# Two token groups hand the last two of their eight units to a fourth block of fast products

## The chip, the cores and the metric

The kernel runs on one core of a Trainium2 chip. The metric is the device time of one execution in microseconds (us). The engines are TensorE (PE, matmuls, with its weight loads as PEld), VectorE (DVE), ScalarE (ACT), GpSimd (POOL) and SyncE (SP), which issues nearly all DMAs. Each engine works through its own queue in order.

## What is computed

Attention with a window and with a dilated window for 8 batches, 8 heads, 576 positions and a head size of 64, then a gated MLP over the 4608 tokens of width 512, with 2048 hidden values:

```python
rel = pos[:, None] - pos[None, :]
mask_plain = (rel >= 0) & (rel < window)                       # window = 32
mask_dil = (rel >= 0) & (rel < window * dilation) & (rel % dilation == 0)
...
attn = np.exp(scores)
attn = attn / (np.sum(attn, axis=-1, keepdims=True) + 1e-09)
return np.matmul(attn, v).astype(np.float32)
...
h = x @ w_in
g = h * (1.0 / (1.0 + np.exp(-1.702 * h)))
return (g @ w_out).astype(np.float32)
```

## The kernel before

The sums are kept in float32 by splitting each operand into a high and a low part: a product is three matmuls (high by high, low by high, high by low) of 128x128 weights and 512 columns.

**Tokens.** Each batch has 576 tokens. The first 512 of a batch make a group of 512 columns; the last 64 of all eight batches make a ninth. Attention is done in 32 pieces k, four for a batch (k = 4b to 4b + 3, two heads each): `scores` (PE, into the bank sp), mask, maximum, subtraction and sum (DVE), exponential (ACT), division (POOL or DVE), transposes (DVE), eight copies into the one buffer bt (ACT or DVE), `product` (PE, into the bank av) and the copy of x out of the bank. In a row of the profile sp is the scores and av the product.

**Groups.** `ALONE` is 3: the groups of batches 0, 1 and 2 (class `Group`, names m0, m1, m2) are multiplied directly. The 2048 hidden values are NF = 16 chunks f of 128. For a chunk, `up` makes hp with 12 matmuls (line 863), ACT and DVE make the gate (lines 871 and 872) and split it into gh and gl, and `Down.pieces` multiplies it onto the four banks acc with 12 matmuls (lines 800, 801, 804). After the last chunk `add_out` stores the group's result. While PE multiplies a chunk, the other engines do the attention of later batches.

**Weight sums.** After group 0, `sum_weights` and `sum_out_weights` make, for each of the PAIRS = 8 units u (chunks u and u + 8 together), the seven combinations of the weights that the blocks need, and store them to DRAM (`sums`, `sums_o`). They work in the arena units 0 to 3 and 4 to 7, one unit u after the other. The eighth (u = 7) adds over wi_last.

**Blocks.** The other six groups are multiplied two at a time by class `Block`: p has the batches 3 and 4, q has 5 and 6, r the ninth group and 7. With two groups of tokens and two chunks of hidden values a product of 2x2 parts is made by seven products in place of eight. `sum_tokens` loads the tokens from `tokens_x`, sums them and splits the seven sums into `wi_kept`, two slots each. The sums for p use the arena units 0 to 11, so the units of the weight sums have to be free, and the slots of wi_kept need every weight sum to be done. Then `products_` goes through the eight units: `up` (42 matmuls a unit, line 1006, seven loads of 256 KB from `sums`), gates, `operands` (sums and splits into wo_kept), and after every second unit `second_products` (84 matmuls, line 1121, seven loads of 512 KB from `sums_o` through a ring of four slots). `add_to` adds the banks to the result units on DVE (line 1142) and stores a finished one.

**Order.** Nothing is scheduled by hand: every step is given to `Plan` with its cost on each engine that can do it and its urgency. `placed` puts the steps in an order by these costs, choosing the engine that would finish first; `latest` gives each step a due time from that order, and three more rounds place them by due times. So the order of all engines is one list made ahead, and each engine's queue is fixed in it.

Of the kernel before, what the change touches and what calls it, by code (L numbers as in the profile page):

```python
# [17 lines left out]
P = 128  # L18
# [5 lines left out]
ALONE = 3  # L24
NSUM = 14
# [191 lines left out]
def tile_windowed_attention_then_gated_mlp(  # L217
# [64 lines left out]
    tokens_x = dram.tile([B * NC, P, GT], F32, tag="tokens_x", name="tokens_x")  # L282
    tokens_r = dram.tile([NC, P, B * LT], F32, tag="tokens_r", name="tokens_r")
# [329 lines left out]
    def drain_x(k, urgency):  # L613
# [53 lines left out]
        if b >= ALONE:  # L667
            add({DMA: 262}, urgency, lambda e: load(tokens_x[k], to), [f"{name}.{n}" for n in range(5)], (f"tx{k}",))
# [115 lines left out]
    class Down:  # L784


        def __init__(self, name, dest):
            self.name, self.dest = name, dest
            self.acc = {}

        def pieces(self, f, high, low, need):
# [4 lines left out]
            def hi(j):  # L796
                if f == 0:
                    self.acc[j] = quarter(j, f"acc_{self.name}_{j}")
                cols = slice(P * j, P * j + P)
                T.matmul(self.acc[j], w[:, 0, cols], high, start=f == 0, stop=False)  # L800
                T.matmul(self.acc[j], w[:, 1, cols], high, start=False, stop=False)  # L801

            def lo(j):
                T.matmul(self.acc[j], w[:, 0, P * j:P * j + P], low, start=False, stop=f == NF - 1)  # L804
# [7 lines left out]
            if f != NF - 1:  # L812
# [3 lines left out]
        def add_out(self, j):  # L816
# [5 lines left out]
            def store(e):  # L822
                load(dst, arena[:, at].rearrange("p (b s) -> p b s", b=dst.shape[1]))

            add({ACT: 0.48, DVE: 0.6}, -9.0, drain, (f"acc{j}",), own(at))
            add({DMA: 262}, -9.0, store, (f"A{at}",), ())
# [5 lines left out]
    class Group:  # L832


        def __init__(self, name, dest):
            self.name = name
            self.g, self.hps = {}, {}
            self.down = Down(name, dest)
# [115 lines left out]
    class Block:  # L954


        def __init__(self, name, sources, dests, units, few=False):
            self.name, self.sources, self.dests, self.few = name, sources, dests, few
# [126 lines left out]
        def second_products(self, chunk):  # L1085
# [14 lines left out]
            def groups(b, n, place, begins, to):  # L1100
                slot = None

                def half(j):
# [4 lines left out]
                    key, fresh = keys[where][j], begins and (where != "R" or chunk == 0)  # L1108
# [49 lines left out]

        def products_(self):


            for u in range(PAIRS):
                self.up(u)
                ops = self.operands(u)
                if u % 2 == 0 and u:
# [35 lines left out]
    for i in range(4):  # L1201
# [3 lines left out]
    main = [Group(f"m{b}", dests[b]) for b in range(ALONE)]  # L1205
# [4 lines left out]
              Block("r", (B, 7), (dests[B], dests[7]), late_units)]  # L1210
# [11 lines left out]
    for b, g in enumerate(main):  # L1222
# [16 lines left out]
        for f in range(NF):  # L1239
# [6 lines left out]
    for block in blocks:  # L1246
        block.sum_tokens()
        if block.few:
# [64 lines left out]
```

## Time and profile before

| | |
|---|---|
| time, median of 3 runs | 823.12 us (821.65 to 823.53) |
| the profiled execution | 822.45 us, span 820.7 us |
| PE busy | 809.3 us, 99% of the span |
| DVE, ACT, POOL busy | 669.0, 518.0, 328.4 us |
| granted TensorE clock | 0.997 |
| DMA | 188.13 MB in the span, 229 GB/s on average |

The span is the time from the first to the last instruction. Busy times of engines overlap. In a row of the timeline the columns are the start and the length in us, the engine, the line of the kernel, the operation, what is written and read, the count, and in brackets the idle time before it with what ended it. In the windows, each engine's busy microseconds and count stand in the order PE, PEld, DVE, ACT, POOL, then the granted clock, the DMA engines' busy share and GB/s.

### The profile page before, as it was taken

The numbers are of one execution on the slowest core, as the hardware profiler recorded it, in microseconds if no ns is written. First come the engines' busy times: TensorE is split into PE (matmuls) and PEld (weight loads), VectorE is DVE, ScalarE is ACT, GpSimd is POOL, SyncE is SP. The second block draws the span as 40 slices with busy tenths as digits, with TensorE's granted clock in tenths as the row PEclk, the third lists the DMA queues.
The fourth block names the chain that finished last, engine by engine and source line by source line (L and its number), as shares of the span: only waits on it lengthen the run. The fifth ranks groups of instructions, "written<-read, shape, count | busy, mean of one in ns | idle before, by whom it ended". The sixth has DMA issues, their size and how long they took to land.

```text
span 820.7 us, 18890 instructions
## 1 busy us (share of the span) xinstructions
PE 809.3 (99%) x7279; PEld 653.4 (80%) x7279; DVE 669.0 (82%) x1081; ACT 518.0 (63%) x988; POOL 328.4 (40%) x294
## 2 busy tenths in 40 slices
PE   7999999999999999999999999999999999999997
PEld 4677878888887888778888888888888888888886
DVE  6898988888888876899889899996679885867575
ACT  7898986767577766786866654545456534544340
POOL 3442325455556553244345445531215332112251
PEclk9999999999999999999999999999999999999999
DMA  9577658899758657797788777775565658674545
GB/s 354 186 249 212 175 161 296 287 318 303 241 176 271 223 180 243 252 307 234 235 236 264 253 254 249 234 256 183 179 207 189 198 189 275 201 226 157 180 153 181
DMA packets 109610, 188.13 MB, mean 229 GB/s; under 512 B 26448, under 2 KB 55376, under 8 KB 109520
## 3 DMA queue, kind: packets, MB, share of 16 engines
q1 hardware_dynamic: 109376, 186.78, 70.2%
q8 instruction: 58, 0.95, 0.5%
q14 instruction: 32, 0.26, 0.1%
q10 hardware_dynamic: 144, 0.13, 0.0%
HBM read 140.64 MB, written 45.09 MB: 226 GB/s over the span
## 4 chain that ended last, share of the span: by engine, by line
PE 97%; DMA 1%; DVE 1%; issue 0%; ACT 0%; SPq 0%; DVEq 0%
PE hp_m L863 16%; PE up_p L1006 10%; PE up_r L1006 9%; PE up_q L1006 9%; PE acc_m L800 5%; PE second_p_Q L1121 5%; PE second_q_Q L1121 5%; PE acc_m L804 5%; PE acc_m L801 5%; PE second_r_Q L1121 5%; PE sp L490 4%; PE second_q_Z L1121 3%; PE second_r_Z L1121 3%; PE second_R L1121 3%; PE second_p_Z L1121 3%; PE av L608 2%
## 5 line engine op out<-in xcount | busy, mean ns | idle before, releaser
L353 POOL TENSOR_TENSOR arena<-arena 128x256 f32<-128x256 f32 (+3 forms) x94 | 100.7, 1083 | 97.8 <-DVE wi_last_units L353 21.6
L863 PE MATMUL hp_m<-xs,wi_kept 128*128 128x512 f32 x504 | 127.7, 396 | 1.2 <-DVE arena L872 0.9
L863 PEld LDWEIGHTS hp_m<-xs,wi_kept 128*128 128x128 f32 x504 | 92.9, 188 | 22.8 <-DVE arena L872 1.9
L353 POOL TENSOR_TENSOR wo_kept<-arena,wo_kept 128x512 fp32r<-128x512 f32 x41 | 56.9, 1395 | 131.5 <-ACT wo_kept L346 84.9
L346 ACT ACTIVATE wo_kept<-arena 128x512 fp32r<-128x512 f32 x111 | 69.2, 630 | 40.7 <-PE second_r_Q L1121 10.9
L1006 PE MATMUL up_r<-wi_kept,xs 128*128 128x512 f32 x336 | 85.3, 389 | 0.0
L1006 PE MATMUL up_p<-wi_kept,xs 128*128 128x512 f32 x336 | 84.2, 394 | 0.2 <-DVE arena L353 0.2
L1006 PE MATMUL up_q<-wi_kept,xs 128*128 128x512 f32 x336 | 83.4, 389 | 0.0
L1006 PEld LDWEIGHTS up_p<-wi_kept,xs 128*128 128x128 f32 x336 | 62.1, 188 | 14.7 <-DVE arena L353 0.9
L1006 PEld LDWEIGHTS up_q<-wi_kept,xs 128*128 128x128 f32 x336 | 63.0, 188 | 13.3 <-DVE arena L1028 0.3
L1006 PEld LDWEIGHTS up_r<-wi_kept,xs 128*128 128x128 f32 x336 | 63.1, 188 | 13.1
L353 DVE TENSOR_TENSOR wo_kept<-arena,wo_kept 128x512 fp32r<-128x512 f32 x80 | 61.1, 775 | 5.1 <-ACT wo_kept L346 4.7
L346 ACT ACTIVATE bt<-ct 32x256 f32<-32x256 f32 (+1 forms) x130 | 56.6, 435 | 11.7 <-DVE ct L534 6.0
L353 POOL TENSOR_TENSOR pr<-pr,sm 128x320 f32<-128x320 f32 x52 | 43.7, 856 | 48.5 <-DVE sm L518 43.5
L800 PE MATMUL acc_m<-gh,wo_kept 128*128 128x512 f32 x156 | 61.5, 394 | 0.0
L353 POOL TENSOR_TENSOR wo_kept<-wi_last_units,wo_kept 128x512 fp32r<-128x512 f32 x22 | 29.9, 1361 | 78.3 <-ACT wo_kept L346 72.3
L353 DVE TENSOR_TENSOR arena<-arena 128x512 f32<-128x512 f32 (+1 forms) x75 | 59.1, 797 | 2.7 <-ACT arena L346 1.8
L801 PE MATMUL acc_m<-gh,wo_kept 128*128 128x512 f32 x156 | 60.8, 390 | 0.0
L1027 ACT ACTIVATE arena<-arena 128x512 f32<-128x512 f32 x60 | 37.4, 628 | 33.4 <-DVE arena L353 27.2
L1028 DVE SCALAR_TENSOR_TENSOR arena<-arena 128x512 f32<-128x512 f32 x60 | 49.8, 837 | 1.7 <-ACT arena L1027 1.3
L346 ACT ACTIVATE gh<-arena 128x512 fp32r<-128x512 f32 x57 | 36.0, 631 | 17.5 <-DVE arena L872 5.8
L353 DVE TENSOR_TENSOR gl<-arena,gh 128x512 fp32r<-128x512 f32 x53 | 41.3, 779 | 6.5 <-ACT gh L346 3.2
(267 smaller groups left out, 1824.7 us busy)
## 6 DMA issues: line engine op xcount, KB each, us to landing
xs<-sums SPq DMA_DIRECT2D x168, 256.0 KB, 3.3
out_weights<-sums_o SPq DMA_DIRECT2D x63, 512.0 KB, 3.5
qk<-qk_dram SPq DMA_DIRECT2D x29, 576.0 KB, 4.4
xs<-sums_o SPq DMA_DIRECT2D x21, 512.0 KB, 3.8
v<-vp_dram SPq DMA_DIRECT2D x28, 320.0 KB, 4.1
sums_o<-arena SPq DMA_DIRECT2D x32, 256.0 KB, 3.2
sums<-arena SPq DMA_DIRECT2D x32, 256.0 KB, 2.9
arena<-wi_dram SPq DMA_DIRECT2D x15, 512.0 KB, 4.7
```

Source lines behind the costliest of these rows:

```text
L346: A.activation(dst, src, AF.Copy, scale=scale)
L353: (V if e == DVE else G).tensor_tensor(out=dst, in0=a, in1=b, op=op)
L490: T.matmul(dst[:, w:w + n], u["qk"][rows, at:at + 32], u["qk"][rows, S + first:S + first + n], start=not masked(k), stop=True, tile_positi ...
L608: T.matmul(u["x"][i][rows, at:at + last - first], u["v"][keys, a, m], bt[keys, m, a, first:last], start=(bank_, a) not in begun, stop=True ...
L800: T.matmul(self.acc[j], w[:, 0, cols], high, start=f == 0, stop=False)
L801: T.matmul(self.acc[j], w[:, 1, cols], high, start=False, stop=False)
L804: T.matmul(self.acc[j], w[:, 0, P * j:P * j + P], low, start=False, stop=f == NF - 1)
L863: T.matmul(hps[f], wi(f)[:, st, cols], mv[:, c], start=c == 0 and k == 0, stop=c == NC - 1 and k == 2)
L1006: T.matmul(self.banks[place], xs[:, slot, at:at + P], wi_kept[:, 2 * a + c, mv], start=fresh and c == 0 and k == 0, stop=c == 1 and k == 2 ...
L1027: add({ACT: 0.60}, -10.0, lambda e: A.activation(unit(tmp), src(), AF.Tanh, scale=0.851), need, own(tmp))
L1028: add({DVE: -0.70 if need[0][0] == "A" else 0.70}, -10.0, lambda e: V.scalar_tensor_tensor(out=unit(dst), in0=unit(tmp), scalar=1.0, in1=s ...
L1121: T.matmul(self.second[key], w[:, st, cols], mv, start=fresh and y == 0 and k == 0, stop=y == 1 and k == 2, skip_group_check=True)
```

## The change

The groups of batches 1 and 2 leave out the chunks whose unit is 6 or 7 (f = 6, 7, 14, 15; `BOTH` is 2) and store what they have to a new DRAM buffer `partial` in place of the output. Their tokens are now also stored to `tokens_x`, as those of later batches are. A fourth block, s, takes the two groups' tokens through units 6 and 7 alone, by the seven products, after r. `begin_with` loads the partial sums into the result units, so that `add_to` adds to them.

```diff
-        if b >= ALONE:
+        if b > 0:
             add({DMA: 262}, urgency, lambda e: load(tokens_x[k], to), [f"{name}.{n}" for n in range(5)], (f"tx{k}",))
...
             def store(e):
-                load(dst, arena[:, at].rearrange("p (b s) -> p b s", b=dst.shape[1]))
+                if self.part is not None:
+                    load(partial[self.part + j], arena[:, at])
+                else:
+                    load(dst, arena[:, at].rearrange("p (b s) -> p b s", b=dst.shape[1]))
...
+            self.fs = [f for f in range(NF) if b == 0 or f % PAIRS < PAIRS - BOTH]
+            self.down = Down(self.name, dests[b], self.fs, NC * (b - 1) if b else None)
...
+        def begin_with(self, first):
+
+
+            for q in range(4):
+                for j in range(2):
+                    at, n = RESULTS[q][j], first + NC * (q // 2) + 2 * (q % 2) + j
+                    self.touched.add((q, j))
+                    add({DMA: 262}, -3.0, lambda e, at=at, n=n: load(unit(at), partial[n]), (f"part{n}",), own(at))
...
-            for u in range(PAIRS):
+            for u in self.us:
...
-              Block("r", (B, 7), (dests[B], dests[7]), late_units)]
+              Block("r", (B, 7), (dests[B], dests[7]), late_units),
+              Block("s", (1, 2), (dests[1], dests[2]), late_units, us=range(PAIRS - BOTH, PAIRS))]
...
-        for f in range(NF):
+        for f in g.fs:
             g.up(f)
...
+        if block is blocks[-1]:
+            block.begin_with(0)
```

The rest of the diff passes the first and last chunk of a group on to the banks' start and stop, and lets block s begin its banks R at its own first pair of units. Since the planner makes the order anew, it changes from group 1 on. Lines of the changed kernel are 3 to 7 higher than those of the kernel before (1006 is now 1013, 608 is 611, 353 is 356).

**The entry into block p on PE.** Before, the queue has this where group 2 ends and p begins; acc_m2 belongs to group 2, up_p_0_0 and up_p_0_1 are the first products of p:

```order
L800 MATMUL acc_m2_3_3497<-gh1_74,wo_last_71 128x512
L801 MATMUL acc_m2_3_3497<-gh1_74,wo_last_71 128x512
L804 MATMUL acc_m2_0_3484<-gl1_76,wo_last_71 128x512
L804 MATMUL acc_m2_1_3487<-gl1_76,wo_last_71 128x512
L804 MATMUL acc_m2_2_3493<-gl1_76,wo_last_71 128x512
L804 MATMUL acc_m2_3_3497<-gl1_76,wo_last_71 128x512
L800 MATMUL acc_m2_0_3484<-gh0_73,wo_last_71 128x512
L801 MATMUL acc_m2_0_3484<-gh0_73,wo_last_71 128x512
L1006 MATMUL up_p_0_0_4600<-wi_kept_68,xs_72 128x512 x6
L1006 MATMUL up_p_0_1_4611<-wi_kept_68,xs_72 128x512 x3
L800 MATMUL acc_m2_1_3487<-gh0_73,wo_last_71 128x512
```

The products of p begin while the group's last chunk and a half still have to be multiplied onto acc. In the changed kernel the rows ahead of up_p are these; the last acc_m2 stands 15 rows above the first of them, right behind the matmuls of sp_24 and av_22, with sp_25 and av_23 and the first two rows of av_24 between:

```order
L611 MATMUL av_24_4296<-bt_77,v_24_4260 64x96 x10
L611 MATMUL av_24_4296<-bt_77,v_24_4260 64x64 x2
L611 MATMUL av_24_4296<-bt_77,v_24_4260 64x32 x2
L611 MATMUL av_24_4296<-bt_77,v_24_4260 64x64 x4
L493 MATMUL sp_26_4333<-qk_26_4266 32x64 x36
L611 MATMUL av_25_4393<-bt_77,v_25_4325 64x96 x2
L611 MATMUL av_25_4393<-bt_77,v_25_4325 64x32 x2
L611 MATMUL av_25_4393<-bt_77,v_25_4325 64x96 x10
L611 MATMUL av_25_4393<-bt_77,v_25_4325 64x64 x2
L611 MATMUL av_25_4393<-bt_77,v_25_4325 64x32 x2
L611 MATMUL av_25_4393<-bt_77,v_25_4325 64x64 x4
L1013 MATMUL up_p_0_1_4434<-wi_kept_68,xs_72 128x512 x3
```

No multiplication of a group is left between; the pieces 24 and 25 of attention stand ahead of p.

**The same place on DVE.** Before, the sums and splits of p's tokens (arena from arena, wi_kept from arena) stand among the gates of group 2's chunks 14 and 15 and one mask of attention:

```order
L353 TENSOR_TENSOR wi_kept_68<-arena_78,wi_kept_68 128x512
L353 TENSOR_TENSOR arena_78<-arena_78 128x512
L872 SCALAR_TENSOR_TENSOR arena_78<-arena_78,hp_m2_14_4459 128x512
L534 STREAM_TRANSPOSE ct1_92<-pr1_84 128x2x5x32
L353 TENSOR_TENSOR pr0_83<-sp_26_4487,mask_97 128x2x4x64
L534 STREAM_TRANSPOSE ct1_92<-pr1_84 128x2x5x32
L353 TENSOR_TENSOR pr0_83<-sp_26_4487,mask_97 64x2x64
L510 TENSOR_REDUCE mx0_85<-pr0_83 128x10
L353 TENSOR_TENSOR wi_kept_68<-arena_78,wi_kept_68 128x512
L353 TENSOR_TENSOR gl0_75<-arena_78,gh0_73 128x512
L353 TENSOR_TENSOR arena_78<-arena_78 128x512
L353 TENSOR_TENSOR wi_kept_68<-arena_78,wi_kept_68 128x512
```

In the changed kernel the last of the weight sums' adds (arena from wi_last) is followed by the mask of sp_24, and the work of attention piece 24 by that of 25 and 26:

```order
L356 TENSOR_TENSOR gl1_76<-arena_78,gh1_74 128x512
L356 TENSOR_TENSOR arena_78<-arena_78 128x512
L356 TENSOR_TENSOR arena_78<-wi_last_69 128x512
L356 TENSOR_TENSOR pr0_84<-sp_24_4079,plain_99 128x2x4x64
L356 TENSOR_TENSOR pr0_84<-sp_24_4079,plain_99 64x2x64
L513 TENSOR_REDUCE mx0_86<-pr0_84 128x10
L351 COPY arena_78<-av_22_4116 128x2x16
L351 COPY arena_78<-sp_24_4079 128x16 x2
L356 TENSOR_TENSOR pr0_84<-pr0_84,mx0_86 128x10x64
L351 COPY bt_77<-arena_78 32x8x32
L353 TENSOR_SCALAR arena_78<-acc_m2_2_3068 128x512
```

42 instructions further on from the mask of sp_24, the first split that a product of p waits for is the first of the four in this piece:

```order
L356 TENSOR_TENSOR pr0_84<-pr0_84,mx0_86 128x10x64
L356 TENSOR_TENSOR wi_kept_68<-arena_78,wi_kept_68 128x512
L529 TENSOR_REDUCE sm0_89<-pr0_84 128x10
L356 TENSOR_TENSOR arena_78<-arena_78 128x512
L521 RECIPROCAL sm0_89<-sm0_89 128x10
L356 TENSOR_TENSOR arena_78<-arena_78 128x512
L356 TENSOR_TENSOR wi_kept_68<-arena_78,wi_kept_68 128x512 x4
L537 STREAM_TRANSPOSE ct0_92<-pr0_84 128x2x5x32 x2
L356 TENSOR_TENSOR wi_kept_68<-arena_78,wi_kept_68 128x512
L356 TENSOR_TENSOR arena_78<-arena_78 128x512
L356 TENSOR_TENSOR wi_kept_68<-arena_78,wi_kept_68 128x512
```

No gate of a group is among them any more; the mask of sp_24, at the head of the 42, reads matmuls that stand just ahead of the last acc_m2.

**The end on SP.** Before, the last loads of weights for r (out_weights, xs) are followed by the stores of the results and by nothing else:

```order
L1096 DMA out_weights_4830<-sums_o_80 128x1024 x3
L1096 DMA xs_72<-sums_o_80 128x1024
L1096 DMA out_weights_4830<-sums_o_80 128x1024 x3
L1096 DMA xs_72<-sums_o_80 128x1024
L1096 DMA out_weights_4830<-sums_o_80 128x1024
L1157 DMA out_dram<-arena_78 1024x1x64 x2
L1157 DMA out_dram<-wi_last_units_4743 128x512 x2
L1157 DMA out_dram<-arena_78 1024x1x64 x2
```

Now the stores of r's results, the loads of partial sums into the same units and the loads of weights for s stand among each other:

```order
L1164 DMA out_dram<-wi_last_units_4602 128x512 x2
L1173 DMA arena_78<-partial_82 128x512
L1173 DMA wi_last_units_4602<-partial_82 128x512
L1103 DMA xs_72<-sums_o_80 128x1024
L1173 DMA wi_last_units_4602<-partial_82 128x512
L1164 DMA out_dram<-arena_78 128x512 x2
L1103 DMA out_weights_4183<-sums_o_80 128x1024
L1164 DMA out_dram<-arena_78 1024x1x64 x2
L1173 DMA arena_78<-partial_82 128x512
L1103 DMA out_weights_4183<-sums_o_80 128x1024
L1173 DMA arena_78<-partial_82 128x512
L1103 DMA out_weights_4183<-sums_o_80 128x1024
```

A load of a partial sum follows the store of r's result from the same unit, and three loads of weights stand behind such loads.

More of the change, by code (lines that the diff above doesn't have):

```diff
@@ L24 @@
 ALONE = 3
+BOTH = 2
 NSUM = 14
@@ L282, in tile_windowed_attention_then_gated_mlp @@
     tokens_x = dram.tile([B * NC, P, GT], F32, tag="tokens_x", name="tokens_x")
+    partial = dram.tile([2 * NC, P, GT], F32, tag="partial", name="partial")
     tokens_r = dram.tile([NC, P, B * LT], F32, tag="tokens_r", name="tokens_r")
@@ L784, in tile_windowed_attention_then_gated_mlp, with __init__ @@
     class Down:
-        def __init__(self, name, dest):
-            self.name, self.dest = name, dest
+        def __init__(self, name, dest, fs, part=None):
+            self.name, self.dest, self.fs, self.part = name, dest, fs, part
             self.acc = {}
@@ L810, in add_lo @@
                 add({PE: 0.227}, 0.0, lambda e: lo(j), (key, need[1]), (f"acc{j}",), count=2)
[L812 removed]
+            if f != self.fs[-1]:
                 return [lambda j=j, piece=piece: piece(j) for piece in (add_hi, add_lo) for j in range(NC)]
@@ L822, in store @@
             def store(e):
-                load(dst, arena[:, at].rearrange("p (b s) -> p b s", b=dst.shape[1]))
+                if self.part is not None:
+                    load(partial[self.part + j], arena[:, at])
+                else:
+                    load(dst, arena[:, at].rearrange("p (b s) -> p b s", b=dst.shape[1]))
             add({ACT: 0.48, DVE: 0.6}, -9.0, drain, (f"acc{j}",), own(at))
-            add({DMA: 262}, -9.0, store, (f"A{at}",), ())
+            add({DMA: 262}, -9.0, store, (f"A{at}",), () if self.part is None else (f"part{self.part + j}",))
     def split(src, high, low, need, to, urgency, costs=split_costs, slack=0.0):
@@ L1107, in half @@
                     where = "Z" if place == "R" and self.few else place
-                    key, fresh = keys[where][j], begins and (where != "R" or chunk == 0)
+                    key, fresh = keys[where][j], begins and (where != "R" or chunk == self.us[0] // 2)
                     def work(e, y):
@@ L1204, in tile_windowed_attention_then_gated_mlp @@
     dests = [tokens[:, b:b + 1, 0:GT] for b in range(B)] + [tokens[:, :, GT:S]]
-    main = [Group(f"m{b}", dests[b]) for b in range(ALONE)]
+    main = [Group(b) for b in range(ALONE)]
     early_units = [(4 * c, 4 * c + 1, 4 * c + 2, 4 * c + 3, 10 + c) for c in range(2)]
```

17 lines of the change are left out of this document (8 added, 9 removed).

## The prediction

> **What bounds the kernel now.** I read the page first: its span, the busy line and the shares of the chain that ended last.
>
> ```profile
> span 820.7 us, 18890 instructions
> PE 809.3 (99%) x7279; PEld 653.4 (80%) x7279; DVE 669.0 (82%) x1081; ACT 518.0 (63%) x988; POOL 328.4 (40%) x294
> PE 97%; DMA 1%; DVE 1%; issue 0%; ACT 0%; SPq 0%; DVEq 0%
> ```
>
> PE is busy all the time and carries the chain, so a matmul left out is time won, as long as PE is never made to wait. Whether it waits today is in the list of waits. Its rows for the multiplications of the groups and of block p are these two:
>
> ```profile
> PE hp_m L863 <- DVE arena L872: 0.9, 1, 0.9
> PE up_p L1006 <- DVE arena L353: 0.2, 1, 0.2
> ```
>
> PE waits for the other engines some 1 us in the whole main part. That does not mean that they have room. The table of windows gives the busy time of each engine up to the end of group 0, through groups 1 and 2, through block p and the start of q, and to the end:
>
> ```profile
> 0.00:118.00 118.00, 111.64 (x1727) 83.85 (x1728) 101.67 (x191) 104.62 (x177) 41.12 (x46) 0.99 0.70 229
> 118.00:338.00 220.00, 219.91 (x2848) 178.50 (x2847) 179.05 (x311) 156.88 (x341) 118.67 (x125) 1.00 0.76 254
> 338.00:545.00 207.00, 206.82 (x1517) 168.06 (x1517) 189.83 (x284) 130.24 (x260) 96.62 (x71) 1.00 0.77 248
> 545.00:821.00 276.00, 270.88 (x1192) 222.98 (x1190) 198.45 (x298) 126.23 (x212) 72.02 (x52) 1.00 0.61 195
> ```
>
> The third busy column is DVE: 179.05 of 220 us in groups 1 and 2, 189.83 of 207 (92%) in the stretch after, 198.45 of 276 (72%) at the end. Before block p DVE has almost as much to do as PE; the end has room. The change takes PE work out of the first and puts it into the last.
>
> **Products.** The chain gives what one matmul of 512 columns costs when they follow each other:
>
> ```profile
> 176.59 2.72 PE hp_m L863 x12
> 474.91 2.72 PE up_p L1006 x12
> 472.19 2.72 PE second_p_Q L1121 x12
> ```
>
> 2.72 / 12 = 0.227 us, the same for all three kinds. Removed: 4 of 16 chunks in two groups, 12 matmuls up and 12 down each, 2 x 4 x 24 = 192, or 43.5 us, all ahead of p. Added: block s, 2 units x 42 up and 84 down, 168 matmuls, 38.1 us, at the end. The difference is 24 x 0.227 = **-5.4 us**. The other engines lose 8 gates and their splits and gain block s's sums, gates, splits and drains; these lie in the last stretch beside matmuls, at nothing, because DVE has 77 us free there (276 - 198.45). Were that cover gone, each DVE operation of 512 elements would cost 0.69 us.
>
> **The entry into p.** This is the term that decides. What must be done before p is not reduced: eight units of weight sums, the attention of tokens 3 and 4, and the 14 splits into wi_kept. Their own pace before, from the issues of SP, the adds of DVE, the splits of POOL, and the first start in up_p's row:
>
> ```profile
> 294.84 2.52 SPq L899 DMA_DIRECT2D sums<-arena  x4
> ...
> 315.83 1.18 SPq L899 DMA_DIRECT2D sums<-arena  x2
> ...
> 320.64 2.40 SPq L974 DMA_DIRECT2D arena<-tokens_x  x4
> ```
>
> ```profile
> 300.74 0.68 DVE L353 TENSOR_TENSOR arena<-wi_last 128x512 f32<-128x512 f32 x1
> ```
>
> ```profile
> 329.11 2.64 POOL L353 TENSOR_TENSOR wi_kept<-arena,wi_kept 128x512 fp32r<-128x512 f32 x2 [2.23 <-ACT wi_kept L346]
> ```
>
> ```profile
> L1006 PE MATMUL up_p<-wi_kept,xs x336: 387/389/501, 337.9 to 477.2; 128*128 128x512 f32 x168
> ```
>
> The seventh and eighth unit's sums are stored 21 us apart; the tokens can be loaded only when the eighth has left the same arena units; the first splits end at 331.75, 31.0 us after the add over wi_last. PE noticed none of it: it had group 2's last chunks to multiply until 337.9.
>
> In the new order PE has no such work. After the matmuls of sp_24 come four of acc_m2, the last of the group, then only attention (sp_25 with av_23, av_24, sp_26, av_25), and then up_p. On DVE's queue, in order, 42 instructions stand from the mask of sp_24, which cannot start before sp_24's matmuls, to the split on which the first product of p waits. Their prices, from the timeline of DVE:
>
> ```profile
> 305.66 0.26 DVE L348 COPY arena<-sp 128x16 f32<-128x16 f32 x2
> 311.20 0.22 DVE L518 RECIPROCAL sm<-sm 128x10 f32<-128x10 f32 x1
> 313.93 0.28 DVE L353 TENSOR_TENSOR pr<-sp,plain 64x128 f32<-64x128 f32 x1 [0.41 <-ACT arena L346]
> 314.25 0.82 DVE L510 TENSOR_REDUCE mx<-pr 128x10 f32<-128x640 f32 x1
> 318.12 0.90 DVE L534 STREAM_TRANSPOSE ct<-pr 128x320 f32<-128x320 f32 x2
> 320.97 0.64 DVE L348 COPY bt<-ct 32x320 f32<-32x320 f32 x2
> 328.66 0.69 DVE L353 TENSOR_TENSOR arena<-arena 128x512 f32<-128x512 f32 x1
> ```
>
> 13 of 512 elements at 0.69 (9.0), 9 passes over 640 at 0.82 (7.4), 4 transposes at 0.45 (1.8), 4 copies into bt at 0.32 (1.3), 3 masks of 64x128 at 0.28 (0.8), 3 reciprocals at 0.22 (0.7), 6 small copies at 0.13 (0.8): 21.8 us. PE's work beside it, by these pieces of the chain:
>
> ```profile
> 323.45 0.91 PE acc_m L804 x4
> ...
> 324.81 0.95 PE av L608 x37
> ...
> 329.17 0.90 PE sp L490 x58
> ```
>
> 0.91 + 2 x 0.90 + 3 x 0.95 + 3 x 0.227 = 6.2 us. PE waits at least 21.8 - 6.2 = 15.6 us before its first product is through. The next 19 DVE instructions (16 x 0.69 + 0.9 + 0.28 = 12.2 us) stand ahead of av_26, with 18 x 0.227 + 0.9 = 5.0 us of PE work: 7.2 more. So the floor is **22.8 us**, if DVE never idles; a tenth off the prices makes it 19. For the other end, DVE's share in the same place before:
>
> ```profile
> 296.00:338.00 42.00, 42.00 (x506) 33.88 (x504) 31.18 (x56) 30.07 (x68) 18.90 (x19) 1.00 0.79 269
> ```
>
> 31.18 of 42 is 74%: 34.0 / 0.74 = 45.9 us against 11.2 of PE, **34.7 us**. At the 92% of the next stretch it is 37.0 - 11.2 = 25.8. The chain of the eighth unit agrees: in the new order its add over wi_last stands on DVE right ahead of the mask of sp_24, so p starts 31.0 us later, against 5.5 us of PE work: 25.5. I take **+26**, between the two. ACT (30.07 of 42) and POOL (18.90) are lower and no ends. What is late next is p itself: the weights' sums for it are then done, so I add nothing there.
>
> **Waits inside the wait.** In the first microseconds PE stood still once, and the clock column shows what followed:
>
> ```profile
> 18.40:20.90 2.50, 0.67 (x57) 0.63 (x55) 1.28 (x5) 2.25 (x3) 1.53 (x3) 1.00 1.02 397
> 20.90:24.40 3.50, 3.50 (x84) 1.76 (x66) 3.38 (x7) 2.43 (x7) 1.11 (x1) 0.51 0.81 289
> ```
>
> After a window with 0.67 us of PE work in 2.5 the granted clock was 0.51 for 3.5 us: 1.75 us lost. In the stretch before p most of such loss falls into time in which PE waits anyway; the last one, after the wait, does not. Between 0 and two of them (3.5), I take **+1**. The Trainium skill (TensorE: Matmul & The Clock Gate, Part 1) has the rule: an idle window of about 3.4 us halves the clock until a busy one has passed. By it every gap before av_24, av_25 and up_p would bring a cold start; the trace agrees on the one gap it has. The rule speaks against this change, and the second rival prices it.
>
> **The end.** Blocks r and s use the same result units: a result of r must be stored and its partial sum of s loaded before s can add to it, and on SP's queue loads of weights stand behind these waiting loads. Such transfers, by the page and its windows:
>
> ```profile
> xs<-sums SPq DMA_DIRECT2D x168, 256.0 KB, 3.3
> out_weights<-sums_o SPq DMA_DIRECT2D x63, 512.0 KB, 3.5
> ```
>
> A store and a load follow each other in about 2 x 3.3 = 6.6 us; all of it could show, or none, if r's last results come early enough. The queue has both kinds of neighbours: I take **+3**, half, and keep 0 and 6.6. The stores of tokens 1 and 2 (eight) and of the partial sums (eight) in front are hidden: 16 issues of SP, which nobody awaits there.
>
> **The sum.** The profiled execution took 822.45 us (1.75 around its span), the three runs' median is 823.12 (821.65 to 823.53), so it stands for them. 822.45 - 5.4 + 26 + 1 + 3 = **847**. The floors of all terms: 822.45 - 5.4 + 19 = 836. The ceilings: 822.45 - 5.4 + 34.7 + 3.5 + 6.6 = 862.
>
> **The rivals.**
> First, PE stays busy, and the change does what its count of products says: 822.45 - 5.4 = 817, faster. For it speaks that PE hardly waits today though DVE is at 92% after 338; it needs DVE to be some 23 us further ahead than its own queue lets it be when sp_24 ends. Against it stands the in-order queue: the mask of sp_24 can't run early. Its point of decision is whether any acc_m2 is left when up_p is due; none is. Chance 0.05.
> Second, the clock: all matmuls of the stretch run at 0.51, and none of that hides, because DVE waits in turn for each slow attention product. 11.2 us of PE work then take 11 more: 847 + 11 - 1 = 857. The row at 20.90 speaks for it, against it that PE is not the late one there. The page's rule of the last part would give this. Chance 0.12.
> Third, the wait exists, but the planner's order happens to win nearly as much back by attention done early (av_25 is ahead of up_p, where it stood in p before): PE work that is moved is not saved, so this only pays if p waited for it otherwise, and in the trace it does not (0.2 us). A result within 0.2% of now would need a wait of 4 to 7 us. Chance 0.02.
> That the change doesn't do what it says is excluded by the order: 24 matmuls fewer, no more.
>
> **How the numbers follow.** Forecast 0.81, rivals 0.05, 0.12, 0.02. 0.2% (1.6 us) is about what a measurement of this kernel can tell from no change. Range: from the floor with one more tenth off DVE's prices, 834, to the ceiling, 862. It leaves out the first and the third rival and a part of the second. Faster 0.05, same 0.02, slower 0.93.
>
> **What would show it.** Right: in the list of waits, PE av, sp and up_p against DVE and ACT, 20 to 35 us in sum, all in 295 to 340; the last acc_m2 near 295, up_p's first start at 322 to 333; PE some 803 to 805 us busy; the clock below 1 once or twice there; waits of some us in second_s at the end. Wrong: up_p starting near 303 with no wait; or the waits lying somewhere else, in p, where DVE would be late by its load and not by the entry; or waits of DVE on PE in 295 to 330, with PE busy.

## The result and the profile after

The changed kernel takes 864.57 us (median of 4 runs, 862.42 to 866.43) against 823.04 us (4 runs, 821.65 to 823.53): 1.0507 of the time before, 95% interval 1.0474 to 1.0539. The sign was forecast, the size was not: 847 us, at most 862. The profiled execution took 866.43 us, its span is 864.7. First the page of the changed kernel, the same three rows as of before.

```profile
span 864.7 us, 19074 instructions
PE 817.3 (95%) x7255; PEld 653.8 (76%) x7255; DVE 702.1 (81%) x1138; ACT 529.3 (61%) x1004; POOL 336.2 (39%) x303
PE 55%; DMA 4%; DVE 2%; issue 1%; ACT 1%; SPq 1%; DVEq 0%
```

PE does 24 products fewer and yet is busy 8 us longer, so some of them ran slowly; and only 55% of the chain that ended last is PE, where it was 97%. The windows (us of the window, then busy us of PE, PEld, DVE, ACT, POOL, the granted clock, the share of the transfer engines and GB/s) put the loss in one place:

```profile
118.00:295.00 177.00, 174.55 (x2359) 139.97 (x2357) 146.46 (x250) 120.98 (x270) 97.64 (x106) 1.00 0.80 260
295.00:345.00 50.00, 23.74 (x497) 16.73 (x493) 37.71 (x73) 32.07 (x74) 15.57 (x19) 0.60 0.93 321
345.00:545.00 200.00, 197.38 (x1360) 158.84 (x1360) 177.65 (x274) 122.03 (x237) 85.91 (x65) 1.00 0.73 231
296.00:338.00 42.00, 18.48 (x414) 13.52 (x413) 29.94 (x61) 25.04 (x60) 14.57 (x19) 0.61 0.98 337
```

From 295 to 345 PE stands still for 26.3 us, and its 23.74 busy us ran at a mean clock of 0.60, so that some 9.5 of them are slowness (an estimate, 0.40 x 23.74). The last row is the window that the prediction showed of before (42.00 of 42 busy, DVE 31.18, transfers at 0.79): now PE has 18.48, DVE is no busier (29.94, 71%), and the transfer engines are full (0.98). The list of PE's waits names whom it waits for, in us, times, longest:

```profile
PE av L611 <- ACT arena L349: 8.6, 1, 8.6
PE sp L493 <- ACT arena L349: 5.3, 2, 3.2
PE acc_m L803 <- ACT gh L349: 4.1, 2, 3.6
PE up_p L1013 <- ACT wi_kept L349: 3.2, 1, 3.2
PE second_s_Z L1128 <- DMA out_weights<-sums_o: 2.5, 1, 2.5
PE av L611 <- DMA v<-vp_dram: 2.4, 1, 2.4
PE second_s_Q L1128 <- DMA out_weights<-sums_o: 2.0, 1, 2.0
```

The first four and the sixth lie at the entry into p, the other two in block s. What decides is seen best in dates. These rows are the seventh and eighth unit's stores on SP's queue, the two adds that open the eighth unit on DVE, p's first split, and the products of p (shortest, median, longest ns, then the first and the last start):

```profile
294.14 1.65 SPq L906 DMA_DIRECT2D sums<-arena  x2
296.68 1.33 SPq L906 DMA_DIRECT2D sums<-arena  x2
...
316.87 1.18 SPq L906 DMA_DIRECT2D sums<-arena  x2
...
320.04 1.62 SPq L906 DMA_DIRECT2D sums<-arena  x2
```

```profile
302.55 0.69 DVE L356 TENSOR_TENSOR arena<-wi_kept 128x512 f32<-128x512 f32 x1 [2.27 <-DMA sums<-arena]
...
304.64 0.69 DVE L356 TENSOR_TENSOR arena<-wi_last 128x512 f32<-128x512 f32 x1 [0.20 <-DMA sums<-arena]
```

```profile
330.68 0.69 DVE L356 TENSOR_TENSOR wi_kept<-arena,wi_kept 128x512 fp32r<-128x512 f32 x1 [1.27 <-ACT wi_kept L349]
```

```profile
L1013 PE MATMUL up_p<-wi_kept,xs x336: 387/389/797, 333.5 to 478.4; 128*128 128x512 f32 x168
```

Before, the first split is this one on DVE, ahead of the two on POOL that end at 331.75:

```profile
328.06 0.68 DVE L353 TENSOR_TENSOR wi_kept<-arena,wi_kept 128x512 fp32r<-128x512 f32 x1
```

Before, the seventh unit's sums left at 294.84, the eighth's at 315.83, the first split was done at 328.74, and p's last product started at 477.2. Now these are 294.14, 316.87, 331.37 and 478.4. PE had 43.5 us less to do ahead of them, and not one of the four came more than 0.7 us earlier. So all of the products left out in front were lost: p's last product is due at 477.2 - 43.5 = 433.7 by PE's work and stands at 478.4, 44.7 us late. Behind it the profiled execution of before has 822.45 - 477.2 = 345.3 us left, that of after 866.43 - 478.4 = 388.0: 42.7 more, the 38.1 us of block s and 4.6 of waits. 44.7 + 4.6 - 5.4 = 43.9; measured 43.98.

### The profile page after: what moved, and what is told of

It is laid out like the page before. It is cut to its first block, busy times and chain, and to the rows that moved or that the text cites. A ratio compares the mean times of both kernels' runs of the same rounds, so it can differ in the third digit from the quotient of the medians.

```text
span 864.7 us, 19074 instructions
## 1 busy us (share of the span) xinstructions
PE 817.3 (95%) x7255; PEld 653.8 (76%) x7255; DVE 702.1 (81%) x1138; ACT 529.3 (61%) x1004; POOL 336.2 (39%) x303
## 4 chain that ended last, share of the span: by engine, by line
PE 55%; DMA 4%; DVE 2%; issue 1%; ACT 1%; SPq 1%; DVEq 0%
PE up_q L1013 9%; PE up_r L1013 8%; PE up_p L1013 8%; PE second_r_Q L1128 5%; PE second_q_Q L1128 5%; PE second_p_Q L1128 5%; PE second_R L1128 3%; PE second_r_Z L1128 3%; PE second_q_Z L1128 3%; PE second_p_Z L1128 2%; PE up_s L1013 2%; DMA out_weights<-sums_o 2%; PE second_p_R L1128 1%; DMA arena<-tokens_x 1%; PE second_s_Q L1128 1%
## 5 line engine op out<-in xcount | busy, mean ns | idle before, releaser
L356 POOL TENSOR_TENSOR arena<-arena 128x256 f32<-128x256 f32 (+3 forms) x94 | 96.8, 1038 | 91.0 <-DVE wi_last_units L356 25.9
L870 PE MATMUL hp_m<-xs,wi_kept 128*128 128x512 f32 x456 | 115.9, 396 | 1.6 <-DVE arena L879 1.3
L349 ACT ACTIVATE wo_kept<-arena 128x512 fp32r<-128x512 f32 x124 | 77.3, 630 | 48.6 <-PE second_r_Q L1128 10.0
L870 PEld LDWEIGHTS hp_m<-xs,wi_kept 128*128 128x128 f32 x456 | 83.9, 188 | 21.7 <-DVE arena L879 3.0
L1013 PE MATMUL up_p<-wi_kept,xs 128*128 128x512 f32 x336 | 88.8, 408 | 6.4 <-ACT wi_kept L349 3.2
L356 DVE TENSOR_TENSOR wo_kept<-arena,wo_kept 128x512 fp32r<-128x512 f32 x91 | 69.2, 770 | 5.0 <-ACT wo_kept L349 4.8
L356 POOL TENSOR_TENSOR wo_kept<-wi_last_units,wo_kept 128x512 fp32r<-128x512 f32 x27 | 39.1, 1448 | 84.1 <-ACT wo_kept L349 76.2
L356 POOL TENSOR_TENSOR pr<-pr,sm 128x320 f32<-128x320 f32 x52 | 42.6, 833 | 43.5 <-DVE sm L521 40.2
L803 PE MATMUL acc_m<-gh,wo_kept 128*128 128x512 f32 x140 | 55.8, 398 | 0.5 <-ACT gh L349 0.5
L804 PE MATMUL acc_m<-gh,wo_kept 128*128 128x512 f32 x140 | 54.6, 390 | 0.0
L349 ACT ACTIVATE wo_kept<-wi_last_units 128x512 fp32r<-128x512 f32 x51 | 32.1, 630 | 28.6 <-PE second_q_Z L1128 7.1
L349 ACT ACTIVATE arena<-av 128x256 f32<-128x256 f32 (+8 forms) x68 | 22.0, 387 | 39.5 <-PE sp L611 27.2
```

The costliest lines, as they stand in the source:

```text
L349: A.activation(dst, src, AF.Copy, scale=scale)
L356: (V if e == DVE else G).tensor_tensor(out=dst, in0=a, in1=b, op=op)
L803: T.matmul(self.acc[j], w[:, 0, cols], high, start=f == self.fs[0], stop=False)
L870: T.matmul(hps[f], wi(f)[:, st, cols], mv[:, c], start=c == 0 and k == 0, stop=c == NC - 1 and k == 2)
L1013: T.matmul(self.banks[place], xs[:, slot, at:at + P], wi_kept[:, 2 * a + c, mv], start=fresh and c == 0 and k == 0, stop=c == 1 and k == 2 ...
```

## The experiments

Times are medians, ratios are to the kernel before on the same chip. "Last product of p" is the last start in up_p's row; the time that follows it is 387.7 to 392.9 us in the profiles of all runs with block s.

**Is it the entry, or block s?** Two kernels isolate the ends of the change. e1_no_last drops block s without a substitute:

```diff
-            self.down = Down(self.name, dests[b], self.fs, NC * (b - 1) if b else None)
+            self.down = Down(self.name, dests[b], self.fs)
...
-              Block("s", (1, 2), (dests[1], dests[2]), late_units, us=range(PAIRS - BOTH, PAIRS))]
```

> Left out of the computation: units 6 and 7 of groups 1 and 2, which no block makes up for; groups 1 and 2 end early, the fourth block is gone, PE does 38.1 us less than in the changed kernel. Theory (the loss lies at the entry into p, 37 of some 49 us, and does not depend on the fourth block; 4.5 us of waits lie in that block): 864.6 - 38.1 - 4.5 = 822 us, with PE's delay against its own work still near 45 to 49 us behind the entry. Rival (the loss belongs to the fourth block and what it adds to transfers and engines): the kernel falls to the kernel before less the work left out, 822.5 - 43.5 = 779 us, and the entry is closed.

e2_whole keeps block s and lets the groups do everything:

```diff
-            self.fs = [f for f in range(NF) if b == 0 or f % PAIRS < PAIRS - BOTH]
+            self.fs = list(range(NF))
```

> Units 6 and 7 of groups 1 and 2 are multiplied twice, so the output counts them twice: groups 1 and 2 keep all eight units, still put their sums aside, and the fourth block runs as well. Theory (what is lost is lost because PE runs out of work before the entry into p): the entry is closed as in the kernel before, and the time is the kernel before plus 38.1 us of the block plus 4.5 us of waits in it, 865 us, where 43.5 us more of products than in the changed kernel cost nothing. Rival (the entry is late because of the stores and loads that the change adds, or the new order): its loss stays, 865 + 37 = 902 us.

Measured: e1 824.12 us, ratio 1.001 (1.000 to 1.002); e2 867.09 us, 1.053 (1.051 to 1.055). The products of p in e1, then in e2:

```profile
L1013 PE MATMUL up_p<-wi_kept,xs x336: 387/389/796, 332.4 to 477.0; 128*128 128x512 f32 x168
```

```profile
L1013 PE MATMUL up_p<-wi_kept,xs x336: 387/389/504, 340.0 to 479.7; 128*128 128x512 f32 x168
```

The theory holds in both: with 43.5 us of products left out and nothing added, the kernel is as fast as before; with 43.5 us more than in the changed kernel it is 2.5 us slower. Between these two, PE's work ahead of p costs next to nothing. Block s costs 864.57 - 824.12 = 40.5 us by the one pair, 867.09 - 823.0 = 44.1 by the other, 38.1 of it products.

**How much room was there?** e11_one_unit leaves out a single unit (BOTH = 1), again with no fourth block.

> Groups 1 and 2 leave out only the last of the eight units, and no fourth block makes up for it (unit 7 of groups 1 and 2 is missing from the output): 96 matmuls, 21.8 us, less on PE ahead of p than before, and nothing added. Theory (the other engines had no room at p's entry at all): the time stays at that of the kernel before, 820 to 825 us. Rival, the size that the prediction gave (26 of 43.5 us lost, so 17.5 us of room): 823 - 17.5 = 806 us.

827.19 us, 1.0042 (1.0023 to 1.0061). Already half of the products buys nothing; it even costs some 3 us. The 17.5 us of room that the prediction implied do not exist.

**The clock.** e3_fill puts constant matmuls into the gap:

```diff
+            def spin(e, i):
+                if i == 0:
+                    misc["spin"] = bank([P, GT], "hp", "spin")
+                for _ in range(4):
+                    T.matmul(misc["spin"], ident, ident[:, None, :].broadcast_to([P, GT // P, P]), start=True, stop=True)
+
+            for i in range(26):
+                add({PE: 0.227 * 4}, 0.0, lambda e, i=i: spin(e, i), (), ("hp",), count=4)
```

> All of the computation as in the changed kernel; 104 matmuls of a constant (24 us at full clock) are put on PE where it waits ahead of p, on the bank of the first products, so that the granted clock stays up. Theory (the gap is set by what VectorE and the transfers do; the halved clock costs only where PE's own work is due: 8.8 us of up_p in 333 to 345 at half, and attention's products in the chain): 4 to 9 us less, 856 to 861 us, first up_p within 3 us of 333. Rival A (the clock is hidden under the waits): 864 within 1 us. Rival B (the clock makes most of the gap, each product of the chain taking double): 20 us less or more, 845 us.

859.15 us, 1.0442 (1.0416 to 1.0468), 5.4 us less than the changed kernel. Its window:

```profile
290.00:340.00 50.00, 40.73 (x532) 22.95 (x528) 37.66 (x65) 30.73 (x71) 16.44 (x18) 0.90 0.86 298
```

The size is that of the theory, the dates are not: the eighth unit's stores left at 309.14 instead of 316.87 and the first up_p came at 323.5, outside the 3 us allowed. Full-speed attention products and the planner's new order in the gap cannot be told apart here, so how much of the 5.4 us is the clock stays open.

**The full transfer engines.** e4_late_loads holds back the loads of weights that are not needed first (a key "tokens_in", written by the token loads, is read by them).

> All of the computation; the first block's loads of weights for its products 1 to 5 and of its first out weights (about 2.8 MB of some 17 MB that move from 290 to 340) wait until its tokens have been loaded. Theory of the full transfer engines (share 1.0 at 360 to 374 GB/s, so that stores and token loads in the chain land late): 2.8 MB less ahead of the chain is 7.6 us, the first up_p at 326, 857 us. Rival (VectorE's queue sets the entry): the first up_p stays at 333 within 2 us, and the products behind it wait for their weights instead, 864 to 869 us.

866.43 us, 1.053 (1.0501 to 1.0558): no gain. The share of the transfer engines fell to 0.76, from 0.97 in the same 50 us of the changed kernel; the first product came 14.2 us earlier, the last one 2.8:

```profile
290.00:340.00 50.00, 28.17 (x622) 21.25 (x622) 39.59 (x73) 34.06 (x85) 21.54 (x23) 0.68 0.76 253
```

```profile
L1013 PE MATMUL up_p<-wi_kept,xs x336: 387/389/797, 319.3 to 475.6; 128*128 128x512 f32 x168
```

The prediction of the first start at 326 is passed, and it is worth nothing: a first start is not p's date.

**Attention's place and the tokens' place.** e5_late_attention lets the softmax of attentions 24 and later wait for p's last split; e6_units loads p's tokens into units 10 to 15 and 18 to 21, which the weight sums do not use.

> All of the computation; the softmax of attentions 24 and later waits until p's token sums are all split, so that some 14 us of VectorE's work between 296 and 332 (three attentions' maxima, sums, subtractions, transposes) stand behind the splits. Theory of VectorE's queue (34 us of it ahead of p against 11.2 us of PE's work): the first up_p comes 10 to 14 us earlier, at 320 to 323; the attentions then press p, where VectorE is busy 35 of 40 us, and a part comes back there: 852 to 860 us. Rival (a chain of transfers and single steps sets the entry, VectorE has room in it: it is busy 37.9 of 50 us): the first up_p at 331 to 333, 864 us or up to 5 more.

> All of the computation; the tokens of p are loaded into units of the arena that the weight sums do not use, so that their loads need not wait for the stores of the eighth unit (316.9 and 320.0). Theory of the chain (eighth unit's store, then token load, then sums and splits): one landing of a store and one of a load, 5 to 7 us each, go out of it: the first up_p 8 to 12 us earlier, at 322 to 325, 853 to 857 us. Rival (VectorE's queue): first up_p at 331 to 333, since the same work stands in it, 862 to 865 us.

e5: 875.19 us, 1.0634 (1.0596 to 1.0672), 10.6 us slower; PE waits 20.4 us for p's splits all the same, and the postponed attention presses p and q (last product of p 481.9, of q 638.2 instead of 628.8). e6: 864.93 us, 1.0493 (1.0465 to 1.0522), nothing. Its first product of p starts at 297.0 and its last at 477.2; the weight sums' last stores slipped to 330.38:

```profile
301.66 1.19 SPq L906 DMA_DIRECT2D sums<-arena  x2
304.90 1.32 SPq L906 DMA_DIRECT2D sums<-arena  x2
330.38 1.18 SPq L906 DMA_DIRECT2D sums<-arena  x2
332.86 1.28 SPq L906 DMA_DIRECT2D sums<-arena  x2
```

Both fell as theories of one culprit. Whatever I moved out of the way, p's last product started within 4 us of where it had been.

**VectorE's amount of work.** e7_no_max leaves the row maximum and its subtraction out of softmax:

```diff
-        add({DVE: 0.80}, urgency, lambda e: V.tensor_reduce(out=mx, in_=sp(), axis=AX.X, op=ALU.max),
-            held or (PR,), (MX,))
-        add({DVE: 0.80 if masked(k) else -0.80}, urgency, lambda e: pair(
-            e, pr, sp(), mx[:, :, :, None].broadcast_to([P, 2, QT, W]), ALU.subtract), (*held, MX), (PR,))
-        add({ACT: 0.75}, urgency, lambda e: A.activation(prs[y], prs[y], AF.Exp, scale=0.125), (), (PR,))
+        add({ACT: 0.75}, urgency, lambda e: A.activation(prs[y], sp(), AF.Exp, scale=0.125), held, (PR,))
```

> The changed kernel; its softmax leaves out the search for the row maximum and its subtraction (two VectorE operations, 0.80 and 0.89 us in the trace, in each of 32 attentions), which shifts numerator and denominator alike. 27 attentions lie ahead of p's splits: 27 x 1.69 = 45.6 us of VectorE's work less there, nothing less on PE, 7 MB of transfers and all ScalarE and GpSimd work as before. Theory (VectorE's own work, all of it up to p's last splits, sets when p can run, whatever PE leaves out): the 37 to 45 us at the entry close almost wholly, 822 to 830 us. Rival A (transfers and the chain of the eighth unit): at most 10 us less, 855 or more. Rival B (GpSimd and ScalarE with it): half, about 845 us.

> The changed kernel; maximum and subtraction are left out only in attentions 16 and later, 11 of them ahead of p's splits: 11 x 1.69 = 18.6 us of VectorE's work less there. Theory (VectorE's work in total sets p's time, microsecond for microsecond): 864.6 - 18.6 = 846, within 4 us. Rival (what counts is a threshold or a chain, not the amount): no change, or the whole 40 us as in the full case.

> The kernel before, with the maximum and its subtraction left out of softmax in the same way. PE is 99% busy there, and what VectorE does not do stands beside PE's work: both theories expect 820 to 823 us. Less than 817 would say that PE's busy time itself holds waits that the profile does not show.

e7: 850.76 us, 1.0325 (1.0303 to 1.0346); e9: 862.23 us, 1.0467 (1.0446 to 1.0487); e8: 826.41 us, 1.0037 (1.0022 to 1.0053). My theory of VectorE's amount fell: 45.6 us less of its work gave 13.8, and 18.6 us less gave 2.3, which the intervals don't even separate from nothing. The stores of the weight sums in e7 showed what had moved with the time:

```profile
243.22 2.88 SPq L910 DMA_DIRECT2D sums<-arena  x4
264.75 3.59 SPq L910 DMA_DIRECT2D sums<-arena  x4
286.70 2.72 SPq L910 DMA_DIRECT2D sums<-arena  x4
304.85 3.12 SPq L910 DMA_DIRECT2D sums<-arena  x4
```

Unit follows unit at 18 to 22 us though VectorE has far less to do, and the last one is 12 to 15 us earlier than in the changed kernel, as much as the time. Every unit uses the same eight units of the arena: the next may write there when the last one's stores have landed. The adds of the changed kernel at 302.55 and 304.64 name these stores in their brackets (DMA sums<-arena), though with only 2.27 and 0.20 us of idle time; what fills the rest of a unit's 18 to 22 us was not broken down.

**The chain of weight sums.** e15_seven_sums and e16_six_sums leave out the sums of the last unit and of the last two; e12b_three_areas removes nothing and gives the sums a third area in turn. It also puts the sums' steps at other places in the order: five units behind group 1's first chunk and three behind group 2's. With four and four and all of softmax (e12_three_sets) there is no time: the engines of that kernel wait for each other without end. The areas in e12b:

```diff
+    SETS = (0, 4), (4, 8), (18, 22)
...
-        sum_halves(urgency, (wi(f), wi(g)), (f"wi{f}", f"wi{g}"), range(4),
+        sum_halves(urgency, (wi(f), wi(g)), (f"wi{f}", f"wi{g}"), range(*SETS[2 * u % 3]),
...
-        sum_halves(urgency, (wo(f), wo(g)), (f"wo{f}", f"wo{g}"), range(4, 8),
+        sum_halves(urgency, (wo(f), wo(g)), (f"wo{f}", f"wo{g}"), range(*SETS[(2 * u + 1) % 3]),
```

> The changed kernel without the weight sums of its eighth unit; the blocks multiply by the seventh unit's sums a second time in their place (the output is therefore not that of the reference; PE's products, attention and token sums are all there). Theory of the chain (each unit's sums use the same eight units of the arena, so that they follow each other at 21.6 us, and the eighth ends the wait): 21.6 us less, 843 us within 4. Rival of VectorE's amount of work: one unit is at most 8.8 us of its time (for weights in and out, 2 sums of 0.69, 4 halves of 0.40 and 2 splits of 0.69 each): 856 us or more. Rival of attention as the last to be ready: no change, 864.

> The same without the sums of the seventh and the eighth unit (the sixth's, for weights out the fifth's too, are multiplied in their place). Theory of the chain: another 15 to 21 us less, 822 to 828 us, where other work becomes the limit. Rival of VectorE's amount: 17.6 us less than 864.6 in all, 847 us. Rival of attention: 864.

> All of the computation of the changed kernel; the sixteen sets of weight sums go through three areas of the arena in turn instead of two (units 0 to 3, 4 to 7, 18 to 21; the last three units' sums are recorded behind group 2's first chunk, so that the groups' results, which use 18 to 21 too, come between). No work is taken from any engine. Theory of the chain: the last sums that p needs are stored earlier than 317 to 320, and the time falls by 15 to 25 us, 840 to 850. Rival (VectorE's amount of work): 864 within 3 us.

e15: 854.44 us, 1.0367 (1.0350 to 1.0383). e16: 834.13 us, 1.0124 (1.0108 to 1.0140). e12b: 853.85 us, 1.0368 (1.0341 to 1.0395). p's products in e15, in e16 and in e12b:

```profile
L1013 PE MATMUL up_p<-wi_kept,xs x336: 387/389/795, 308.6 to 465.4; 128*128 128x512 f32 x168
```

```profile
L1013 PE MATMUL up_p<-wi_kept,xs x336: 387/389/796, 295.1 to 446.2; 128*128 128x512 f32 x168
```

```profile
L1014 PE MATMUL up_p<-wi_kept,xs x336: 387/389/796, 312.4 to 465.6; 128*128 128x512 f32 x168
```

With no work taken from any engine the third area and the new places are worth 10.7 us, which VectorE's amount alone cannot explain; no run has the new places with two areas, so their part is not known. One unit of chain gave 10.1, not 21.6, and the second 20.3 more. A second limit that stood fixed some 10 us on would have held back the second unit too, so leaving out sums must relieve both; they are work of VectorE as well. The chain theory's 843, 822 to 828 and 840 to 850 us are missed by 11, 6 and 4 us, and VectorE's 856, 847 and 864 are undercut by 2, 13 and 10: neither is whole by itself.

Nor did the theory's own sign come. The last unit's sums leave later than the 316.87 of the changed kernel, and what comes earlier are the loads of p's tokens, which began at 324.37 there. In e12b, then in e13_sets_no_max (below), the first of these loads and the last unit's stores:

```profile
303.25 0.88 SPq L982 DMA_DIRECT2D arena<-tokens_x  x2
...
321.06 3.44 SPq L907 DMA_DIRECT2D sums<-arena  x4
```

```profile
273.43 1.87 SPq L986 DMA_DIRECT2D arena<-tokens_x  x2
...
330.48 1.18 SPq L911 DMA_DIRECT2D sums<-arena  x2
```

So the date of the last store does not set p's date by itself. But e6 had freed the token loads alone and gained nothing: which link of the chain the third area relieves is not shown.

**Both limits at once.** e13_sets_no_max has the three areas and no maximum; e14_before_sets is the kernel before with the same two cures; e17_areas_no_max_fill adds 40 constant matmuls to e13.

> Three areas for the weight sums, and softmax without the maximum and its subtraction (which leaves the quotient as it is): the chain shortened and 45.6 us less of VectorE's work ahead of p. Theory (two limits of nearly the same length lay under PE's work, the chain of weight sums first and VectorE's queue next): together they close the entry, 818 to 828 us. Rival (something else is the second limit, transfers at a share of 1.0 or ScalarE): above 835 us.

> The kernel before with both cures, three areas for the weight sums and softmax without maximum and subtraction. PE is 99% busy there, so neither can give it much: 820 to 826 us. It is the measure for the changed kernel with the same two cures: the change itself is worth 5.4 us of products less some waits at the end, so that one should be 0 to 6 us faster than this one.

> The changed kernel with three areas, no maximum in softmax, and 40 matmuls of a constant (9 us at full clock) in PE's waits ahead of p. Three areas and no maximum alone gave 831.2 us, with the last 2 to 4 us of it at the end of the fourth block. Theory (what is left at the entry is the clock, at 0.97 from 290 to 340, and two waits of 5 us): 826 to 831 us. Rival (PE's wait is gone, the constant matmuls stand in the way): 832 to 836 us. Less than 823, and so a version that beats both kernels, needs both the entry and the end closed: not expected.

e13: 831.21 us, 1.0087 (1.0069 to 1.0106). e14: 828.08 us, 1.0062 (1.0039 to 1.0086). e17: 831.90 us, 1.0099 (1.0082 to 1.0115). e13 at the entry, and its products of p:

```profile
290.00:340.00 50.00, 44.45 (x502) 33.61 (x501) 44.91 (x77) 35.53 (x74) 22.60 (x20) 0.97 0.88 296
```

```profile
L1018 PE MATMUL up_p<-wi_kept,xs x336: 387/389/797, 294.1 to 443.1; 128*128 128x512 f32 x168
```

The two cures are worth 33.4 us together, more than 10.7 and 13.8 added, as it would be if each alone uncovered the other limit. PE is busy 44.45 of 50 us, and DVE 44.91, 90%, where it had been 37.88. The changed kernel is then 2 to 3 us behind the kernel before with the same cures, with intervals that overlap, so the entry was almost all of its loss: p's last product starts at 443.1 against 479.7 in e14, 36.6 of the 43.5 us saved. e13 came out 3 us above what I had expected. In e17 the clock is at 1.00 in the same window and the time is the same; that speaks against the clock as the rest, but its 40 constant matmuls take some 9 us of PE themselves, and 831.90 lies between the ranges of theory and rival. GpSimd and ScalarE were not relieved by any run alone, though PE's four largest waits name ScalarE, and GpSimd's sums of halves for the eighth unit end at 316.21, right ahead of its first stores. No version beats 823 us. That the cures make the kernel before 3 to 5 us slower was not expected; see the end.

**The end.** e10_no_partial leaves the partial sums unloaded (the call of begin_with is gone).

> The fourth block does not load the partial sums of groups 1 and 2 and so does not add them (the output lacks units 0 to 5 of these groups); all products stay. Theory (the two waits for out weights at the end, 4.5 us, come from the eight loads of partial sums, 2 MB, that stand among them in the queue): 4 to 5 us less, 860 us, and no second_s row in the waits. Rival (the last weights come late by themselves, the block being short): the waits stay, 864 within 1 us.

865.49 us, 1.0496 (1.0456 to 1.0537): no change, and in its list of waits the end still stands:

```profile
PE second_s_Q L1128 <- DMA out_weights<-sums_o: 1.8, 1, 1.8
```

So the eight loads are not what costs the time, though the other wait of block s, 2.5 us, is not in this list. What makes block s wait stays open; 2.4 to 6.0 us (e1's pair and e2's) is its price.

## Why the prediction was right in sign and wrong in size

**The products, -5.4 us: right.** 44.7 + 4.6 - 5.4 gives the measured difference, and the price of block s by e1 and e2 is 38.1 and a few us.

**The entry, +26, and p itself, "I add nothing there": the steps that failed.** The reading of the order was right: PE ran out of group 2's chunks and waited for attention's drains and p's splits. But for these terms and the clock's +1, together 27 us, the runs show 44.7, and they fall into two parts. In the new order 170 of the 192 products fewer stand ahead of p's first product (the other 22 had stood behind it) and one of attention's `product` steps more, as the counts of matmuls in the two traces show, so by PE's work it was due at 337.9 - 38.5 + 1.0 = 300.4. It came at 333.5, 33.1 us late. From there to the last product it took 144.9 us where before it had taken 139.3 with 6.0 us more of PE's work in it, those 22 products and that step of attention: another 11.6 us.

The first part fails in the sentence "in the new order its add over wi_last stands on DVE right ahead of the mask of sp_24, so p starts 31.0 us later, against 5.5 us of PE work". From that add to p's first product it is about that long: 304.64 to 333.5 is 28.9. But the sentence lets the add come when PE is due at sp_24, 300.4 - 5.5 = 294.9. It came at 304.64, 9.7 us later: DVE was busy for 9.80 of the 10 us up to 300 and then waited for the seventh unit's stores, which left from 294 on in both kernels. 28.9 - 5.5 + 9.7 = 33.1. The same holds of the other two estimates: 42 instructions counted on DVE's queue from a moment that was tied to PE's place.

The second part is p itself, which the prediction put at nothing because the weights' sums are then done. The splits behind the first one came one by one, since the tokens' loads for them left from 324.37 to 336.51. From p's first product to its last PE stood still for 5.8 us, and in the first 13 us its clock was 0.50 with 9.58 us busy, which is some 4.8 us of slowness (an estimate). The prediction's own sign of being wrong, waits in p, came in part. e4 and e6 show it more plainly: starts at 319.3 and 297.0, the last product at 475.6 and 477.2.

Most of the answer stood in the rows before: p's first split was done at 328.74, the first three by 331.75, and PE came at 337.9. Some 6 to 9 us lay between, so as long as those dates stay, leaving out more than that of PE's work ahead of p can win nothing, and e11 says that the later splits had not even that.

**DVE's price, 22.8 to 34.7: right for its part.** DVE was 71% busy in that window, as it had been (74%); 34.0 / 0.71 - 11.2 = 36.7. From the mask of sp_24 (306.62) to the end of the first split (331.37) it was busy 18.26 of 24.75 us, 74%. The end of the range that came from the row of the same place was the good one, and I moved away from it towards the 92% of another stretch. Still, VectorE alone did not set the date (e7, e9).

**The clock, +1: too small.** The clock fell to 0.50 from 300 to 305 and in every 5 us from 315 to 345, as the first and the last of these windows show:

```profile
300.00:305.00 5.00, 4.43 (x61) 3.21 (x64) 2.53 (x5) 1.03 (x2) 0.00 (x0) 0.50 1.02 374
...
340.00:345.00 5.00, 4.38 (x79) 2.93 (x79) 4.77 (x9) 4.88 (x11) 0.00 (x0) 0.50 0.52 171
```

PE was busy 4.4 us of 5 and got half the clock, so part of its work took double. That was close to the second rival's condition, all matmuls at 0.51, and the 9.5 us of slowness are near its 11. What they cost the kernel is less sure: filling the gap gained 5.4 us (e3), with another order, while the limits were there, and nothing once they were gone and the clock was at 0.97 anyway (e13 to e17). The rule that the prediction cited (the Trainium skill, TensorE: Matmul & The Clock Gate, Part 1: an idle window of some 3.4 us halves the clock until a busy one has passed) agrees with these rows: PE was busy 1.30 us of the 5 ahead of the first, and the clock was 0.96 in the 5 after it. The second rival's 857 us was nearer than 847, but most of the loss is not the clock: with the clock at 0.90 the kernel still took 859.

**The end, +3 within 0 to 6.6: right in size, the reason not borne out.** 4.6 us in the profiles; the loads of partial sums are not the cause (e10).

**The stores in front, nothing: right within 2.5 us**, by p's last product in e2, 479.7 against 477.2. That the transfer engines were full at the entry (0.98, 337 GB/s) was not foreseen; taking load off them alone did not change the time (e4).

## What to carry to other kernels

An engine that is 99% busy and never waits can still stand on top of a second limit that ends at nearly the same moment: before work is taken from it, look up in the trace the date at which the others have the next stage ready, all of its inputs and not the first alone, and count what is saved only down to that date. Such a date belongs to a chain, and buffers can be links of it: eight units through the same part of the arena at some 22 us each did not show in any share of busy time. The Trainium skill (Trainium Kernel Development and Optimization, Best Practices) advises a second buffer to overlap transfers with computing; here a third area for two streams, with their steps placed anew, was worth 10.7 us with no work removed, and it paid more only together with less work for VectorE.

## What the runs showed of the hardware that was not expected

Taking VectorE's work out of the kernel before made it slower: 1.0037 (e8), with a third area as well 1.0062 (e14). In e14's profile most of the loss is at the start and not at the entry into p. The first 40 us of before, then of e14:

```profile
0.00:40.00 40.00, 34.59 (x896) 22.77 (x897) 29.43 (x65) 33.44 (x52) 17.29 (x25) 0.96 0.72 266
```

```profile
0.00:40.00 40.00, 30.25 (x876) 20.57 (x876) 26.30 (x62) 30.65 (x50) 17.68 (x25) 0.96 0.71 260
```

PE is busy 4.3 us less there, with fewer instructions; the whole span is 5.2 us longer (825.9 against 820.7). Which order or wait does it was not pursued.

At the entry of the changed kernel the transfer engines were full for 5 us at a time:

```profile
325.00:330.00 5.00, 2.59 (x115) 2.38 (x96) 3.64 (x8) 2.64 (x6) 0.00 (x0) 0.50 1.08 374
```

With less of this load in e4 (0.76 over 290 to 340) p's first product came 14.2 us earlier and its last 2.8, and the time was the same within its uncertainty: 374 GB/s at a share of 1.08 was not what set it. Why the share exceeds 1 was not pursued.
